# Queries and keys brought to channels by DMA transposes of bfloat16 parts, in a fused mLSTM and feed-forward kernel

## The chip, the cores and the metric

The kernel runs on 1 core of a Trainium2 chip. Its time is the device time of one execution in microseconds (us), given as the median of several runs. A profile of one more execution says what each engine did: PE is the matrix engine (TensorE; PEld its weight loads), DVE the vector engine, ACT the scalar engine, POOL the GpSimd engine, SP the engine that issues nearly all DMAs here (its queue is shown as SPq).

## The reference

An mLSTM layer in its recurrent form (batch 4, 8 heads, 768 tokens, 40 channels a head), then a feed-forward layer without biases on the 3072 tokens of 320 channels (inner width 2048).

```python
for t in range(S):
    m_new = np.maximum(f_gate[:, :, t] + m, i_gate[:, :, t])
    f_stab = np.exp(f_gate[:, :, t] + m - m_new); i_stab = np.exp(i_gate[:, :, t] - m_new); m = m_new
    C = f_stab[..., None, None] * C + i_stab[..., None, None] * np.einsum('bhd,bhe->bhde', vt, kt)
    n = f_stab[..., None] * n + i_stab[..., None] * kt
    h_tilde = np.einsum('bhde,bhe->bhd', C, qt); nq = np.einsum('bhd,bhd->bh', n, qt)[..., None]
    y[:, :, t] = sigmoid(o_gate[:, :, t]) * h_tilde / np.maximum(np.abs(nq), 1.0)
x = y.transpose(0, 2, 1, 3).reshape(B * S, H * D)
h = x @ w_in
out = (np.maximum(h, 0.0) + alpha * np.minimum(h, 0.0)) @ w_out
```

## The kernel before

The recurrence is computed in chunks of 128 tokens: 6 chunks (`NC`) for each of 4 batches, so chunks n = 0 to 23, with c = n % 6 the place in the batch. In a chunk the scores of all 8 heads are a product of keys and queries over the 40 channels (`pS`), weighed by the decays `E`, and multiplied by the values (`pH`). What came before the chunk enters by the state `C_t` (keys by values, 40 x 42 a head: 40 values, and two columns for the denominator), multiplied by the queries (`pI`, none where c is 0); `update` brings the state on (`pu`, none where c is 5). Two chunks make a group g of 256 tokens; the feed-forward of a group runs in 8 steps `fp`: `up` (16 matmuls of 256 columns into `ph`, of an activation and weights that are each split into a high and a low part), ACT and DVE form the activation, ACT and POOL split it (`gh`, `gl`), and two steps later `down` (12 matmuls of 320 columns into `po`).

The Python generators set only the order in which the program is written: `attention` yields pieces, and `side.until` places them between the feed-forward's steps. A scheduler then fixes one order for each engine, and every engine works through its own order strictly in sequence. On SP that goes for DMAs too: a DMA whose wait is not over holds all DMAs behind it.

Queries and keys arrive by token, `qn_t` and `kn_t` of [128 tokens, 8 heads, 64], two buffers each. The matmuls contract over partitions, so both are brought to channels in `stage_a`: four transposes of pairs of heads each (`transposed`, L176: `pq` and `pk` in PSUM), in float32. Up to chunk 6 (`NDIR` is 7) the result is used in float32. From chunk 7 on `stacked` makes of each a stack of 120 partitions: the high part rounded to float32r by ACT (`qh`, `kh`, L184), the rest by DVE or POOL (`kl`, `ql`), and six DMAs of 40 partitions by 512 elements each (L192) lay high, low and high below one another, so that one float32r matmul a head (L369) gives the scores to nearly float32. For the state product the queries are also kept in float32 (`qf`, L221), and `from_state` does two heads at a time in float32 (L302: four matmuls, each seen by the profile as two).

From chunk 8 on (`NBF`) scores and values are split into three bfloat16 parts for `pH` (`score_parts`, `value_parts`, `values_by_parts`). `open_gate` (L119) takes the sigmoid of the output gates of a whole batch; it stands behind the last chunk of the batch before, right after the DMAs that load the gates.

Of the kernel before, what the change touches and what calls it, by code (L numbers as in the profile page):

```python
# [8 lines left out]
F32 = mybir.dt.float32  # L9
# [8 lines left out]
def kernel(ctx: ExitStack, tc: tile.TileContext, q, k, v, i_gate, f_gate, o_gate, w_in, w_out, alpha, out):  # L18
# [59 lines left out]
    wT = const.tile([P, NC, BH], F32, tag="wT", name="wT")  # L78
    ones = const.tile([BH, R], F32, tag="ones", name="ones")
# [9 lines left out]
    def load_qk(n):  # L89
        b, c = divmod(n, NC)  # L90
        t0 = c * P
        nc.sync.dma_start(qn_t[n % NQ][:, :, :D], q[b, :, t0 : t0 + P, :].rearrange("h p d -> p h d"))
        nc.sync.dma_start(kn_t[n % NQ][:, :, :D], k[b, :, t0 : t0 + P, :].rearrange("h p d -> p h d"))

# [33 lines left out]
    def weighed(n):  # L128

        b, c = divmod(n, NC)  # L130
        kd = sb.tile([P, H, D], F32, tag="kd", name=f"kd{n}")
        (nc.gpsimd if n in KDP else nc.vector).tensor_tensor(
            kd, kn_t[n % NQ][:, :, :D], wT[:, c, b * H : (b + 1) * H].unsqueeze(2).broadcast_to([P, H, D]), ALU.mult
        )
        kds[n] = kd
# [6 lines left out]
    def update_steps(n):  # L142
# [9 lines left out]
        for h in range(H):  # L152
            r = slice(64 * (h % 2), 64 * (h % 2) + D)
            nc.tensor.matmul(pu3[r, h], kd[:, h], va[:, h], start=True, stop=True)  # L154
        yield
        old, new = C_t[(n - 1) % 3], C_t[n % 3]
        if c > 0 and n in CP:
# [13 lines left out]
        yield  # L171

    def transposed(ps, src):
        src = src.rearrange("p h e -> p (h e)")
        for p in range(NPR):
            nc.tensor.transpose(ps[:R, p * P : (p + 1) * P], src[:, p * P : p * P + R], ident)  # L176

    def stacked(ps, nm, n, low, copy=None):


        X = sb.tile([3 * D, 2, 512], F32R, tag=f"{nm}S", name=f"{nm}S{n}")
        Xh = sb.tile([P, 512], F32R, tag=f"{nm}h", name=f"{nm}h{n}", bufs=1)
        Xl = sb.tile([P, 512], F32R, tag=f"{nm}l", name=f"{nm}l{n}", bufs=1)
        nc.scalar.copy(Xh[:R], ps[:R])  # L184
        if copy is not None and n in QLP:
            nc.gpsimd.tensor_tensor(Xl[:R], copy[:R], Xh[:R].bitcast(F32), ALU.subtract)
        else:
            nc.vector.tensor_tensor(Xl[:R], ps[:R], Xh[:R].bitcast(F32), ALU.subtract)
        for par in range(2):
            for j in range(3):  # L190
                src = (Xl if j == low else Xh)[64 * par : 64 * par + D]
                nc.sync.dma_start(X[j * D : (j + 1) * D, par].bitcast(F32), src.bitcast(F32))  # L192
        return X

# [18 lines left out]
    def stage_a(n):  # L213

        c = n % NC
        pq = psa(f"pq{n}")
        transposed(pq, qn_t[n % NQ])
        Q = K = qf = None
        if c > 0 or n < NDIR:
            qf = sb.tile([P, 512], F32, tag="qf", name=f"qf{n}")  # L220
            nc.scalar.copy(qf[:R], pq[:R])  # L221
        if n >= NDIR:
            Q = stacked(pq, "q", n, 1, qf)
        yield
        pk = psa(f"pk{n}")
        transposed(pk, kn_t[n % NQ])
        if n >= NDIR:
            K = stacked(pk, "k", n, 2)
        else:
            K = padded(n)  # L230
            padded_copy(K, pk)
        chunk[n] = (pre.pop(n), Q, K, qf)
        yield
        update(n)
        if n >= NBF:
            for _ in value_parts(n):
                pass
        yield

# [54 lines left out]

    def from_state(n, qf):

        b, c = divmod(n, NC)
        pI = psa(f"pI{n}")
        C = C_t[(n - 1) % 3][:R].rearrange("p h e -> p (h e)")
        for p in range(NPR):  # L300
            es = slice(2 * p * VA, 2 * (p + 1) * VA)
            nc.tensor.matmul(pI[:, es], qf[:R, p * P : (p + 1) * P], C[:, es], start=True, stop=True)  # L302
# [37 lines left out]
    def stage_b(n):  # L340

        b, c = divmod(n, NC)
        Lb, Q, K, qf = chunk.pop(n)
        Es = []
        for par in range(2):
# [9 lines left out]
            for p in range(NPR):  # L355
# [7 lines left out]
                compare_op=ALU.is_ge, fill=0.0,  # L363
            )
            pS = psa(f"pS{n}_{par}")
            for p in range(NPR):
                sl = slice(p * P, (p + 1) * P)
                if n >= NDIR:
                    nc.tensor.matmul(pS[:, sl], K[:, par, sl], Q[:, par, sl], start=True, stop=True)  # L369
                else:  # L370
                    nc.tensor.matmul(pS[:, sl], K[:R, par, sl], qf[:R, sl], start=True, stop=True)
# [8 lines left out]
        if c > 0:  # L380
            *_, T = from_state(n, qf)
        hv = values(n, Es) if n < NBF else values_by_parts(n, Es)
# [55 lines left out]
    def attention(n0):  # L438

        late = iter(())  # L440
        for _ in stage_a(n0):
            yield
        for n in range(n0, B * NC):
            loads(n + 2)
            a = stage_a(n + 1) if n + 1 < B * NC else iter(())
            bb = stage_b(n)
            for part in (a, bb, late, a, bb, a, bb):
                next(part, None)
                if part is not late:
                    yield  # L450
            if n % GC == GC - 1:
                late = stage_x(n // GC)
        for _ in late:
            yield
# [11 lines left out]
    XNP = range(2, 8)  # L466
    QLP = range(6, 24)
    KDP = range(1, 24)
# [11 lines left out]
    class FeedForward:  # L480
# [9 lines left out]
        def up(self):  # L490
# [24 lines left out]
            if g == 1:  # L515
                gh, gl = (
                    sb.tile([P, 2, GT], F32R, tag="qk"[fp % 2] + x, name=f"g{x}{g}_{fp}", bufs=1) for x in "hl"
                )
            else:
# [198 lines left out]
    def first_group():  # L718
# [31 lines left out]
        nc.gpsimd.memset(ones, 1.0)  # L750
        for C in C_t:
# [103 lines left out]
        def warm(n=1):  # L855
# [7 lines left out]
        lf = [  # L863
            sb.tile([P, 512], F32, tag="qk"[j] + "h", name=f"g_lf{j}", bufs=1)[:BH, : (GT, S - GT)[j]] for j in range(2)
        ]
# [159 lines left out]
        )  # L1025
        pg = psa("pg")
        nc.tensor.matmul(pg[:R, : BH * NC], ones, gd.rearrange("p a c -> p (a c)"), start=True, stop=True)
        nc.vector.tensor_copy(gamB[:R].rearrange("p a c -> p (a c)"), pg[:R, : BH * NC])
# [90 lines left out]
```

## Time and profile before

| | us |
|---|---|
| three runs | 515.08, 519.91, 520.13; median 519.91 |
| profiled execution | 517.3 |
| its span, first to last instruction | 515.6 |
| PE busy in the span | 497.3 (96%) |
| DVE, ACT, POOL busy | 340.1, 307.2, 243.6 |
| first and last score matmul from stacks (L369) | starts at 144.2 and 443.7 |

Matmuls are pipelined: the duration of one in the profile (0.27 us for a transpose) is longer than the time until the next one starts. What a group of matmuls costs PE is therefore read from start to start.

### The profile page before, as it was taken

Reading aid. Unit: us, or ns where it says so; the run is one execution under the profiler, and the core shown is the slowest. Engines: PE = TensorE matmul, PEld = TensorE weight load, DVE = VectorE, ACT = ScalarE, POOL = GpSimd, SP = SyncE. Lnnn points to the kernel's source line nnn. Section 1 sums busy time; section 2 is a strip of 40 time slices with the busy share of each in tenths; the row PEclk is TensorE's granted clock in tenths of the full one; section 3 lists DMA queues with packets and bytes.
Section 4 is the critical chain, followed back from the end, with each engine's and each line's share of the span. In section 5 each row is a group of like instructions: output and inputs, shape, how many; then the busy total and the mean of one; then the engine's idle time right before and its main releaser. Section 6 shows DMA issues by size and latency. Waiting matters only on the chain.

```text
span 515.6 us, 11550 instructions
## 1 busy us (share of the span) xinstructions
PE 497.3 (96%) x4335; PEld 483.4 (94%) x4335; DVE 340.1 (66%) x667; ACT 307.2 (60%) x638; POOL 243.6 (47%) x286
## 2 busy tenths in 40 slices
PE   8889889999999999999899999999999999999997
PEld 7778879999999999999799999999999999999997
DVE  7879999745544777773586686685786587552321
ACT  3868697545456566574885666566875664433332
POOL 6632362210276366554666647464766645333242
PEclk9989988999999999999899999999999999999999
DMA  9989986070265454367356464356543121000000
GB/s 171 230 179 270 236 207 176 3 144 27 63 168 138 117 147 111 88 161 140 78 160 133 110 146 130 96 132 132 144 129 99 65 77 40 1 27 0 27 1 26
DMA packets 137999, 58.39 MB, mean 113 GB/s; under 512 B 102792, under 2 KB 126360, under 8 KB 137944
## 3 DMA queue, kind: packets, MB, share of 16 engines
q1 hardware_dynamic: 137864, 57.56, 46.4%
q8 instruction: 34, 0.56, 0.5%
q14 instruction: 21, 0.17, 0.1%
q10 hardware_dynamic: 80, 0.11, 0.1%
HBM read 36.90 MB, written 4.03 MB: 79 GB/s over the span
## 4 chain that ended last, share of the span: by engine, by line
PE 76%; DVE 7%; ACT 5%; DMA 4%; issue 3%; SPq 2%; POOL 2%; ACTq 0%; DVEq 0%; POOLq 0%
PE po L530 28%; PE ph L499 4%; PE ph L502 4%; PE ph L503 4%; PE ph L506 4%; PE ph L500 4%; PE ph L505 4%; PE ph L501 4%; PE ph L504 4%; PE pI L302 3%; DMA og<-in_o_gate_dram 3%; PE pH L285 3%; PE pS L369 2%; SPq L115 2%; PE pu L154 2%
## 5 line engine op out<-in xcount | busy, mean ns | idle before, releaser
L522 POOL TENSOR_TENSOR gl<-g,gh 128x512 fp32r<-128x512 f32 x80 | 103.5, 1295 | 76.0 <-ACT gh L521 64.4
L530 PE MATMUL po<-OH,gh 128*128 128x320 f32 x384 | 116.7, 316 | 1.6 <-ACT gh L521 1.6
L530 PE MATMUL po<-OL,gh 128*128 128x320 f32 x384 | 114.4, 310 | 0.0
L512 DVE SCALAR_TENSOR_TENSOR g<-g,oma,ph 128x256 f32<-128x256 f32 x160 | 69.5, 475 | 62.7 <-ACT g L508 62.2
L508 ACT ACTIVATE g<-ph 128x512 f32<-128x512 f32 x96 | 57.5, 599 | 65.7 <-PE ph L506 60.8
L521 ACT CAST gh<-g 128x512 fp32r<-128x512 f32 x80 | 49.6, 620 | 51.8 <-DVE g L512 51.1
L530 PEld LDWEIGHTS po<-OH,gh 128*128 128x128 f32 x384 | 72.4, 189 | 2.4 <-ACT gh L521 2.1
L530 PE MATMUL po<-OH,gl 128*128 128x320 f32 x384 | 73.6, 312 | 0.0
L530 PEld LDWEIGHTS po<-OL,gh 128*128 128x128 f32 x384 | 72.4, 189 | 0.2 <-DVE OL L629 0.2
L530 PEld LDWEIGHTS po<-OH,gl 128*128 128x128 f32 x384 | 60.0, 188 | 0.4 <-POOL gl L522 0.2
L499 PE MATMUL ph<-XH,WH 128*128 128x256 f32 x192 | 59.4, 309 | 0.0
L357 ACT ACTIVATE E<-Lb,bT 128x128 f32<-128x128 f32 x160 | 49.9, 392 | 15.8 <-PE pH L285 13.8
L503 PE MATMUL ph<-X,W 128*128 128x256 f32 x192 | 54.8, 287 | 0.0
L501 PE MATMUL ph<-XH,WL 128*128 128x256 f32 x192 | 54.6, 285 | 0.0
L506 PE MATMUL ph<-X2L,W 128*128 128x256 f32 x192 | 54.5, 285 | 0.0
L500 PE MATMUL ph<-XH,WH 128*128 128x256 f32 x192 | 54.5, 284 | 0.0
L502 PE MATMUL ph<-XH,WL 128*128 128x256 f32 x192 | 54.4, 284 | 0.0
L505 PE MATMUL ph<-XL,WH 128*128 128x256 f32 x192 | 54.3, 283 | 0.0
L504 PE MATMUL ph<-XL,WH 128*128 128x256 f32 x192 | 54.3, 283 | 0.0
L272 ACT CAST E<-pS 128x512 bf16<-128x512 f32 x64 | 37.5, 585 | 19.7 <-DVE pS L270 10.3
L361 POOL TENSOR_SCALAR_AFFINE_SELECT E<-E 128x512 f32<-128x512 f32 x44 | 31.2, 712 | 36.2 <-ACT E L357 35.2
L499 PEld LDWEIGHTS ph<-XH,WH 128*128 128x128 f32 x192 | 36.7, 191 | 0.7
(177 smaller groups left out, 1114.0 us busy)
## 6 DMA issues: line engine op xcount, KB each, us to landing
Lb<-L_d SPq DMA_DIRECT2D x20, 512.0 KB
qS<-qh SPq DMA_DIRECT2D x68, 80.0 KB
kS<-kh SPq DMA_DIRECT2D x68, 80.0 KB
wo<-in_moe_w_out_dram SPq DMA_DIRECT2D x8, 640.0 KB
wi<-in_moe_w_in_dram SPq DMA_DIRECT2D x8, 512.0 KB
qn<-in_q_dram SPq DMA_DIRECT2D x24, 160.0 KB
kn<-in_k_dram SPq DMA_DIRECT2D x24, 160.0 KB
va<-in_v_dram SPq DMA_DIRECT2D x24, 160.0 KB
```

The source lines that it names most:

```text
L499: nc.tensor.matmul(dst, WH[half][:, 0, hs], XH[:, 0], start=True, stop=False)
L500: nc.tensor.matmul(dst, WH[half][:, 1, hs], XH[:, 1], start=False, stop=False)
L501: nc.tensor.matmul(dst, WL[half][:, 0, hs], XH[:, 0], start=False, stop=False)
L502: nc.tensor.matmul(dst, WL[half][:, 1, hs], XH[:, 1], start=False, stop=False)
L503: nc.tensor.matmul(dst, W2[:, fs], X2, start=False, stop=False)
L504: nc.tensor.matmul(dst, WH[half][:, 0, hs], XL[:, 0], start=False, stop=False)
L505: nc.tensor.matmul(dst, WH[half][:, 1, hs], XL[:, 1], start=False, stop=False)
L506: nc.tensor.matmul(dst, W2[:, fs], X2L, start=False, stop=True)
L508: nc.scalar.activation(gt, ph, AF.Relu, scale=-1.0)
L512: nc.vector.scalar_tensor_tensor(out=y[:, e], in0=gt[:, e], scalar=oma[:, f : f + 1], in1=ph[:, e], op0=ALU.mult, op1=ALU.add)
L522: (nc.vector if g < 2 else nc.gpsimd).tensor_tensor(gl, y, gh.bitcast(F32), ALU.subtract)
L530: nc.tensor.matmul(po[j], x[:, e, j * P : (j + 1) * P], W[f // NB][:, f % NB], **ends)
```

## The change

From chunk 7 on TensorE transposes nothing for queries and keys. `stage_s(n + 2)`, two chunks ahead, splits each of them by token into three bfloat16 parts in one tile `Z` of [128 tokens, 2 blocks, 8 heads, 128 places], each block holding 3 x 40 channels and 8 zeros. One DMA transpose on SP's queue turns the 16 blocks of 128 x 128 into a stack `X` of [128 places, 16, 128 tokens] of bfloat16 (512 KB). Block 0 and block 1 hold the parts in two orders, such that two bfloat16 matmuls of 120 partitions a head, block 1 - s of one stack against block s of the other, give six of the nine products of parts.

From batch 1 on the state is kept on 40 partitions (one buffer, `C_t[0]`, updated in place), split into three bfloat16 parts, and laid out as a stack by three plain DMAs (L207 to L209); `from_state` then does two bfloat16 matmuls of 42 columns a head with the query stack. The state of chunk n is split for n = 6 to 22 without c = 5, so 15 times. `qf` is no longer made from chunk 7 on. `open_gate(b)` moves into the first chunk of batch b itself. The feed-forward of group 1 uses the tiles `sp0`, `sp1` that later hold `Z`; `Z` has one buffer for queries and one for keys.

```diff
-    def stacked(ps, nm, n, low, copy=None):
-        X = sb.tile([3 * D, 2, 512], F32R, tag=f"{nm}S", name=f"{nm}S{n}")
...
-                nc.sync.dma_start(X[j * D : (j + 1) * D, par].bitcast(F32), src.bitcast(F32))
+    def token_parts(n, j):
+        src = by_token_of(n, j)
+        Z = sb.tile([P, 2, H, P], BF16, tag=f"sp{j}", name=f"{'qk'[j]}Z{n}", bufs=1)
+        rest = sb.tile([P, H, D], F32, tag="qf", name=f"{'qk'[j]}r{n}")
...
+        nc.gpsimd.memset(Z[:, :, :, 3 * D :], 0.0)
...
+        nc.scalar.copy(both, src.unsqueeze(1).broadcast_to([P, 2, H, D]))
+        (nc.gpsimd, nc.vector)[j].tensor_tensor(rest, src, slot(0, 0), ALU.subtract)
+        yield
+        nc.scalar.copy(slot(1, 1), rest)
+        nc.vector.tensor_tensor(slot(0, 2), rest, slot(1, 1), ALU.subtract)
+        nc.vector.tensor_copy(slot(1 - j, 1 - (1 - j)), slot(0, 0))
+        nc.vector.tensor_copy(slot(j, 1 - j), slot(1, 1))
+        X = sb.tile([P, 2 * H, P], BF16, tag="qk"[j] + "S", name=f"{'qk'[j]}S{n}")
+        nc.sync.dma_start_transpose(X, flat)
...
+    def state(n, pu):
...
+        nc.scalar.copy(X[:D, 0], C)
+        nc.vector.tensor_tensor(rest, C, X[:D, 0], ALU.subtract)
+        nc.scalar.copy(X[:D, 1], rest)
+        nc.gpsimd.tensor_tensor(low, rest, X[:D, 1], ALU.subtract)
+        nc.sync.dma_start(X[D : 2 * D], X[:D])
+        nc.sync.dma_start(X[2 * D : 3 * D, 1], X[:D, 0])
+        nc.sync.dma_start(X[2 * D : 3 * D, 0], low)
...
+            for h in range(H):
+                es = slice(h * VA, (h + 1) * VA)
+                for s in range(2):
+                    nc.tensor.matmul(pI[:, es], Q[: 3 * D, s, h], C[:, 1 - s, es], start=s == 0, stop=s == 1)
...
-                    nc.tensor.matmul(pS[:, sl], K[:, par, sl], Q[:, par, sl], start=True, stop=True)
+                    for s in range(2):
+                        nc.tensor.matmul(
+                            pS[:, sl], K[: 3 * D, 1 - s, h], Q[: 3 * D, s, h], start=s == 0, stop=s == 1
+                        )
...
+            if c == 0 and par == 1:
+                open_gate(b)
...
-            open_gate(b + 1)
...
-            a = stage_a(n + 1) if n + 1 < B * NC else iter(())
+            a = stage_a(n + 1) if n + 1 < NDIR else iter(())
+            far = stage_s(n + 2) if NDIR <= n + 2 < B * NC else iter(())
-            for part in (a, bb, late, a, bb, a, bb):
+            for part in (a, bb, late, far, a, bb, far) + ((a, bb) if n + 1 < NC else (bb, a)):
```

Where the scheduler puts these pieces is seen in the order of each engine. On PE, before, between two steps of group 2's feed-forward (`po2` is the end of one `down`, `ph2_6` the next `up`) stand the query transposes of chunk 9 and half the scores of chunk 8:

```order
L530 MATMUL po2_0_1711<-OH1_873,gl2_3_1927 128x320
L530 MATMUL po2_1_1712<-OH1_873,gl2_3_1927 128x320
L176 MATMUL pq9_2065<-ident_72,qn1_76 104x128 x4
L369 MATMUL pS8_0_2089<-qS8_1792,kS8_1845 128x128 x4
L499 MATMUL ph2_6_2100<-XH2_1683,WH1_553 128x256
```

At the same place now (lines are those of the changed kernel) stand the state update of chunk 8 and twice as many score matmuls, each with a weight load of its own (four of the eight pairs are shown):

```order
L608 MATMUL po2_1_1707<-OH1_871,gl2_3_1927 128x320
L161 MATMUL pu8_2065<-va0_79,kd8_2063 40x42 x8
L443 LDWEIGHTS kS8_1773
L443 MATMUL pS8_0_2103<-qS8_1750,kS8_1773 128x128
L443 LDWEIGHTS kS8_1773
L443 MATMUL pS8_0_2103<-qS8_1750,kS8_1773 128x128
L443 LDWEIGHTS kS8_1773
L443 MATMUL pS8_0_2103<-qS8_1750,kS8_1773 128x128
L443 LDWEIGHTS kS8_1773
L443 MATMUL pS8_0_2103<-qS8_1750,kS8_1773 128x128
```

The transposes are gone there and nothing takes their place; no row of `pq` or `pk` is left from chunk 7 on.

On SP, before, one chunk (17) takes its loads and twelve copies of stack parts:

```order
L99 DMA va0_79<-in_v_dram 128x8x40
L192 DMA qS17_4264<-qh17_4265 40x512 x3
L192 DMA qS17_4264<-ql17_4266 40x512 x2
L192 DMA qS17_4264<-qh17_4265 40x512
L106 DMA Lb19_4577<-L_d_89 128x8x128
L93 DMA kn1_78<-in_k_dram 128x8x40
L99 DMA va0_79<-in_v_dram 128x8x40
L192 DMA kS17_4387<-kh17_4388 40x512 x2
```

Now the same chunk stands there with two transposes, and the three DMAs of the state of chunk 16 behind them:

```order
L244 DMA_TRANSPOSE qS17_4250<-qZ17_4212 128x16x128
L93 DMA kn1_78<-in_k_dram 128x8x40
L244 DMA_TRANSPOSE kS17_4363<-kZ17_4217 128x16x128
L113 DMA Lb19_4727<-L_d_88 128x8x128
L208 DMA C2_87<-C2_87 40x336
L93 DMA qn0_75<-in_q_dram 128x8x40
L207 DMA C2_87<-C2_87 40x672
L106 DMA va0_79<-in_v_dram 128x8x40
L93 DMA kn0_77<-in_k_dram 128x8x40
L209 DMA C2_87<-cw16_4379 40x336
```

The loads of the next chunks (`qn`, `kn`, `Lb`) now stand behind transposes, and each transpose behind the DVE and ACT work on its `Z`.

On ACT, now, the first parts of chunk 10 are written into `Z` between the pieces of group 2's feed-forward step 4:

```order
L427 ACTIVATE E9_1_2449<-Lb9_1799,bT_81 128x128 x4
L235 CAST qZ10_2171<-qn0_75 128x2x8x40
L587 ACTIVATE g2_4_2000<-ph2_4_1983 128x512
L235 CAST kZ10_2176<-kn0_77 128x2x8x40
L599 CAST gh2_4_2004<-g2_4_2000 128x512
L587 ACTIVATE g2_5_2037<-ph2_5_2020 128x512
```

Since `Z` has one buffer, both `L235` rows wait until the transposes of chunk 9 have read it, and `gh2_4` stands behind them.

More of the change, by code (lines that the diff above doesn't have):

```diff
@@ L226, in stage_a, with after @@
         transposed(pk, kn_t[n % NQ])
[L227 to L232, printed above, removed]
+        padded_copy(K, pk)
+        chunk[n] = (None, K, qf)
         yield
+        after(n)
+        yield
+    def after(n):
         update(n)
@@ L237, in stage_a, with stage_s @@
                 pass
+    def stage_s(n):
+        parts = [token_parts(n, j) for j in range(2)]
+        for it in parts:
+            next(it)
+        yield
+        next(parts[0])
+        yield
+        next(parts[1])
+        chunk[n] = (stacks.pop((n, 0)), stacks.pop((n, 1)), None)
         yield
@@ L444, in attention @@
             loads(n + 2)
[L445 removed]
+            a = stage_a(n + 1) if n + 1 < NDIR else iter(())
+            far = stage_s(n + 2) if NDIR <= n + 2 < B * NC else iter(())
             bb = stage_b(n)
[L447 removed]
+            for part in (a, bb, late, far, a, bb, far) + ((a, bb) if n + 1 < NC else (bb, a)):
                 next(part, None)
[L449 removed]
+                if part in (a, bb):
                     yield
+            next(far, None)
+            if NDIR <= n + 1 < B * NC:
+                after(n + 1)
             if n % GC == GC - 1:
@@ L466 @@
     XNP = range(2, 8)
-    QLP = range(6, 24)
     KDP = range(1, 24)
@@ L515, in up @@
             if g == 1:
-                gh, gl = (
-                    sb.tile([P, 2, GT], F32R, tag="qk"[fp % 2] + x, name=f"g{x}{g}_{fp}", bufs=1) for x in "hl"
-                )
+                both = sb.tile([P, 2, 2, GT], F32R, tag=f"sp{fp % 2}", name=f"gg{g}_{fp}", bufs=1)
+                gh, gl = both[:, 0], both[:, 1]
             else:
@@ L863, in first_group @@
         lf = [
-            sb.tile([P, 512], F32, tag="qk"[j] + "h", name=f"g_lf{j}", bufs=1)[:BH, : (GT, S - GT)[j]] for j in range(2)
+            sb.tile([P, 512], F32, tag=f"sp{j}", name=f"g_lf{j}", bufs=1)[:BH, : (GT, S - GT)[j]] for j in range(2)
         ]
```

83 lines of the change are left out of this document (53 added, 30 removed).

## The prediction, written before the changed kernel ran

> **What bounds the kernel now.** I read the busy times first, then the windows (busy us of each engine in a stretch, with the number of instructions), then PE's timeline from start to start.
>
> ```profile
> PE 497.3 (96%) x4335; PEld 483.4 (94%) x4335; DVE 340.1 (66%) x667; ACT 307.2 (60%) x638; POOL 243.6 (47%) x286
> 45.00:110.00 65.00, 60.41 (x494) 57.74 (x493) 57.12 (x108) 48.14 (x107) 22.21 (x27) 0.95 0.70 165
> 145.00:445.00 300.00, 296.96 (x2708) 291.90 (x2707) 207.13 (x400) 190.64 (x406) 171.16 (x193) 0.99 0.46 116
> L369 PE MATMUL pS<-qS,kS 120*128 120x128 f32 x136 | 20.0, 266 | 0.0
> ```
>
> The change touches chunks 7 to 23: 136 score matmuls of 8 a chunk make 17 chunks, and they run from 144 to 444 us. In just this stretch PE is busy 296.96 of 300 us at a granted clock of 0.99, while DVE has 207.13 (69%), ACT 190.64 (64%) and POOL 171.16 (57%). So in the stretch that changes, PE sets the pace; a us of PE work that goes there shortens the run by a us, as long as no other engine steps in. The window 45 to 110 shows what stepping in looks like: DVE at 57.12 of 65 (88%), and PE at 60.41 (93%).
>
> **PE's part of the sum.** These rows are start, duration, line, tile and count; the cost of a group is from its start to that of the next one.
>
> ```profile
> 302.27 0.60 PE L176 MATMUL pq<-ident,qn 128*104 128x128 f32 x4
> 302.71 1.02 PE L302 MATMUL pI<-C,qf 104*128 104x84 f32 x8
> 303.56 0.54 PE L285 MATMUL pH<-vb,E 128*128 128x42 bf16 x10
> 304.15 0.64 PE L285 MATMUL pH<-vb,E 128*128 128x126 bf16 x12
> 304.64 0.36 PE L500 MATMUL ph<-XH,WH 128*128 128x256 f32 x1
> 308.24 0.56 PE L369 MATMUL pS<-qS,kS 120*128 120x128 f32 x4
> 308.63 0.34 PE L499 MATMUL ph<-XH,WH 128*128 128x256 f32 x1
> 43.38 0.38 PE L351 MATMUL pb<-LP,pick 96*128 96x128 bf16 x4
> 43.62 0.38 PE L499 MATMUL ph<-XH,WH 128*128 128x256 f32 x1
> ```
>
> Transposes removed: four take 302.71 - 302.27 = 0.44 us; two such groups in each of 17 chunks: 17 x 0.88 = **-15.0**.
>
> Scores: eight float32r matmuls now, two groups of 308.63 - 308.24 = 0.39, so 0.78 us a chunk. Afterwards 16 bfloat16 matmuls of 128 columns with a weight load each. The nearest row is `pb`, bfloat16 with 96 rows and 128 columns: four in 43.62 - 43.38 = 0.24, 0.06 each, so 0.96. That is 17 x 0.18 = **+3.1**.
>
> State product: 303.56 - 302.71 = 0.85 us now. Afterwards 16 bfloat16 matmuls of 42 columns. The nearest rows are twelve `pH` matmuls of 126, 84 and 42 columns in 304.64 - 304.15 = 0.49: 0.041 each if the weight loads set the pace (16 make 0.65), or 0.49 / 1008 columns x 42 = 0.020 each if columns do (0.33). I take 0.030, 0.48 a chunk, as both kinds stand in that group: 15 chunks have a state product, 15 x 0.37 = **-5.5** (bounds -3.0 and -7.8).
>
> Together -17.4 (-14.9 to -19.7).
>
> **The sigmoid of the gates.** In the trace, ACT waits for a DMA at the second of the three late places:
>
> ```profile
> 243.04 1.28 ACT L119 ACT_TABLE_LOAD   x1 [3.99 <-DMA og<-in_o_gate_dram]
> 246.93 0.57 ACT L415 CAST XH<-p 128x512 fp32r<-128x512 f32 x1
> 248.28 0.67 PE L154 MATMUL pu<-va,kd 128*40 128x42 f32 x16 [2.53 <-DVE XL L418]
> ```
>
> ACT stands 3.99 us for the gates' DMA, its next work (`XH`) is late, DVE's `XL` behind it too, and PE idles 2.53 us. With `open_gate` a chunk later the data lies there: **-2.5**. What is late next at that place is nothing that the trace shows; 0 if some other wait fills the gap.
>
> **The transposes.** No row shows one. They move 512 KB each from SBUF to SBUF. Nearest rows, of SP's queue:
>
> ```profile
> 306.39 2.28 SPq L192 DMA_DIRECT2D qS<-qh  x3
> 311.09 0.43 SPq L106 DMA_DIRECT2D Lb<-L_d  x1
> 305.46 0.84 SPq L99 DMA_DIRECT2D va<-in_v_dram  x1
> qS<-qh SPq DMA_DIRECT2D x68, 80.0 KB
> 258.82 0.87 DVE L563 COPY ob<-po 128x320 f32<-128x320 f32 x2
> 298.07 0.88 DVE L563 COPY ob<-po 128x320 f32<-128x320 f32 x2
> ```
>
> A plain load of as many bytes (`Lb`, 512 KB) holds the queue 0.43 us; the six copies that one transpose replaces (480 KB) hold it 6 x 0.76 = 4.6 us. I take 4.6, the row of the same direction and size, with 0.43 as the lower end and no row for an upper one. A chunk takes 19.6 us (two chunks between the `ob` rows, 39.25). Of it SP needs, at 0.43 to 0.84 an issue, some 2.5 us for loads and stores, 2.3 for the three state DMAs at 0.76, and 9.2 for two transposes: 14.0, not more than the 9.1 + 2.5 of before by much, and it fits. The work they wait for and the work that waits for them (scores) stand some four feed-forward steps apart in PE's order from chunk 8 on, about 14 us. Not so at the start: chunk 7's second half of the scores stands one `up` behind the DVE work that completes `kZ7`. There PE waits for the transpose once: **+4.6** (0.4 to whatever a transpose takes).
>
> [...]
>
> **The other engines.** Rows of the same sizes:
>
> ```profile
> L384 DVE TENSOR_TENSOR T<-T,S 128x336 f32<-128x336 f32 x14 | 11.9, 853 | 0.4
> L384 DVE TENSOR_TENSOR T<-T,pH 128x336 f32<-128x336 f32 x5 | 2.5, 502 | 1.3 <-PE pH L249 1.2
> L924 DVE COPY L_rest<-L 32x256 f32<-32x256 f32 x1 | 0.3, 280 | 0.0
> L563 DVE COPY ob<-po 128x320 f32<-128x320 f32 x22 | 9.9, 479 | 7.6 <-PE po L530 7.6
> L188 DVE TENSOR_TENSOR kl<-pk,kh 104x512 fp32r<-104x512 f32 x17 | 11.6, 684 | 3.6 <-ACT kh L184 3.3
> L625 ACT CAST OH<-t_wo 128x640 fp32r<-128x640 f32 x8 | 5.9, 738 | 2.3 <-DVE t_wo L617 2.0
> L259 ACT CAST vb<-va 128x336 bf16<-128x336 f32 x16 | 7.7, 479 | 0.0
> L184 ACT CAST kh<-pk 104x512 fp32r<-104x512 f32 x17 | 10.1, 592 | 3.4 <-PE pk L176 3.4
> L132 POOL TENSOR_TENSOR kd<-kn,wT 128x320 f32<-128x320 f32 x19 | 14.5, 766 | 45.6 <-DMA kn<-in_k_dram 27.3 <-DVE wT L776 7.9 <-PE pH L285 6.5
> L186 POOL TENSOR_TENSOR ql<-qf,qh 104x512 fp32r<-104x512 f32 x15 | 20.1, 1343 | 31.3 <-ACT qh L184 31.3
> ```
>
> ACT, a chunk: two double casts (0.74 each), two single ones and two of the state (0.48), 3.4, for three of 0.59 that go: 1.6 more, 27 in all, 218 of some 280. POOL: a subtraction of 0.77 and one of the state, two small fills, for `ql` of 1.34: about 0.7 more, 12 in all. Both have room.
>
> DVE does not have much. A chunk gets three subtractions, one of the state (15 of 17 chunks) and four bfloat16 copies of 320 elements, and loses `kl`. A subtraction of two SBUF operands took 0.85 in the late stretch and 0.50 where one operand was in PSUM. A copy is bounded by 0.28 (256 elements, SBUF) and 0.48 (320 from PSUM); I take 0.35. So 3 x 0.85 + 0.75 + 4 x 0.35 - 0.68 = 4.0 us a chunk, 68 in all (39 with 0.50 and 0.28, 77 with 0.85 and 0.48). DVE would have 275 of about 283 us where it had 207 of 300. The order on DVE puts this work between the feed-forward's pairs (`g`, L512), and PE waits for those through `ph` and `gh`. In the window 45 to 110, with DVE at 88%, PE idled 4.6 of 65 us, 7%; at that share the stretch would lose 20 us, but part of those waits came from loads and short chains. I take a loss of 3%, **+8** (0 to 20).
>
> Sum against the profiled execution (517.3, which is 515.6 of span and 1.7 around it, and 2.6 below the median of the runs, 519.91): 517.3 - 17.4 - 2.5 + 4.6 + 8 = 510; with the transposes anywhere below 4.6 a little less. **I forecast 508.**
>
> **Rivals.**
>
> *DVE hides its work after all.* The waits of DVE in the stretch are mostly for PE, and they shrink by themselves when there is more to do. Then the 8 is 0 and the start costs a us or two: 517.3 - 17.4 - 2.5 + 1 = 498.
>
> *DVE becomes the bound.* It decides from 283 - 207 = 76 us of added DVE work in the stretch, 4.5 us a chunk; my upper price is 77. DVE never ran at more than 88% in a long window with this code; 207 + 77 = 284 at 93% is 305 us in place of 300, so 517.3 + 5 - 2.5 = 520: no change, within 512 to 525. Against it: the price at 0.85 already holds the waits for POOL. [...]
>
> *The transposes hold the queue.* Mechanism: SP works in order, and `Z` has one buffer, so ACT's next cast into `Z` waits for the transpose, and `gh` behind it, and PE's `po` behind that. Point: SP is full when two transposes take 18.6 - 4.8 = 13.8 us, 6.9 each. Every us more costs 2 us a chunk, 34 in all: at 8 us 517.3 - 2.5 + 17 x (16.0 + 4.8 - 19.6) = 535, at 10 us 603. For it: no row shows a transpose, and nothing bounds it from above. Against: the same bytes went through the same queue in 9.1 us a chunk. [...]
>
> That the change does not do what it says can be left out: no row of `pq` or `pk` is left in PE's order.
>
> **How the numbers follow.** My forecast (500 to 513) gets 0.46, DVE hidden (about 498) 0.10, DVE bound 0.19, transposes in the way 0.25. A measurement of this kernel can tell about 1% from no change, 5 us: faster means below 514.7. The first two are faster, the third the same, the last slower: 0.56, 0.19, 0.25. The range leaves out the best end of the second and transposes of over 8 us: 496 to 540.
>
> **What would show it.** PE's rows L176 gone from chunk 7 on, score groups of about 0.24 per four matmuls, state products of 0.3 to 0.65. DVE's share in the stretch of the scores: under 92% with PE at 97% or more for the forecast; over 95% with PE waiting for `gh` or `ph` for the second rival. On SP's queue the time of L244: under 5 us each for the forecast; over 7, with ACT's waits L235 behind the transposes, for the third. I am wrong in the sum if the new small matmuls take over 0.1 us each, and in the reasons if PE is full and the time the same.

## The result, and the profile after

The changed kernel takes 545.29 us (four runs, 543.58 to 546.0) against 518.12 for the one before on the same chip: a ratio of 1.0525, with an interval of 1.0456 to 1.0593. It is slower by 5%, where faster by 2% was forecast. The profiled execution took 543.6, its span 541.9.

The changed kernel's page, busy times (with share of the span) and the chain that ended last:

```profile
PE 496.4 (92%) x4455; PEld 473.2 (87%) x4455; DVE 403.2 (74%) x782; ACT 326.7 (60%) x687; POOL 265.8 (49%) x336
...
PE 23%; DVE 20%; DMA 10%; ACT 7%; issue 3%; POOL 2%; ACTq 0%; POOLq 0%; SPq 0%; DVEq 0%
```

Windows of it, two in the stretch with the scores and a short one ahead of it (us of the window, then busy us of PE, PEld, DVE, ACT and POOL, the granted clock, the DMA share, GB/s):

```profile
145.00:445.00 300.00, 271.70 (x2616) 258.73 (x2615) 248.51 (x469) 196.15 (x428) 180.40 (x226) 0.96 0.63 122
400.00:445.00 45.00, 39.84 (x366) 38.06 (x365) 36.56 (x67) 28.97 (x65) 25.48 (x32) 0.89 0.36 71
126.00:129.00 3.00, 3.00 (x17) 2.91 (x17) 0.69 (x1) 0.61 (x2) 0.00 (x0) 0.50 0.66 129
```

In the same 300 us PE had 296.96 us of work before and has 271.70 now. No other engine is full either: DVE has 248.51 (83%). So nothing became the bound; the engines wait for each other, and DMAs now stand in the chain with 10% (4% before).

The granted clock is lower as well: 0.96 in these 300 us, 0.89 in the last 45, against 0.99 before. It is not lower throughout. The trace has it at 0.50 for some 3 us at a time, as in the window from 126 us, which stands behind an idle time of PE of 4.49 us. In that window the matmuls of `ph` start 0.21 us apart (126.17, 126.39, 126.60); at 190.58 and 190.69 it is 0.11. Of PE's eleven idle times of over 1.5 us between 100 and 450 us, seven stand beside such a piece and four do not, and from 300 to 350 us, with PE busy 44.58 of 50, the clock was 1.00. So an idle time alone does not tell when it comes. By the mean clock of the two profiled executions (0.986 in 515.6 us, 0.962 in 541.9) PE lacked some 7 us of full speed before and some 21 now. The difference, 13 us, is an estimate of the most that this took of the 26 us between the two spans. No experiment separates it from the idle time that it goes with.

PE's own work shrank as planned. Start, duration, line, count in the changed kernel:

```profile
155.41 0.57 PE L372 MATMUL pI<-C,qS 120*128 120x42 bf16 x16
155.83 1.96 PE L312 MATMUL pH<-va,E 128*128 128x42 f32 x16
...
165.53 0.62 PE L443 MATMUL pS<-qS,kS 120*128 120x128 bf16 x8
165.96 0.36 PE L578 MATMUL ph<-XH,WH 128*128 128x256 f32 x1
```

Half the scores of a chunk cost 165.96 - 165.53 = 0.43 us (0.39 before), a state product 0.42 (0.85 before). With the 0.88 of the transposes that is 17 x (0.88 - 0.08) + 15 x 0.43 = 20 us less for PE. They are more than lost in two kinds of gaps.

**The landing of the transposes.** The longest waits (in total, times, longest, us) that end with a transpose's landing, and one that hangs on them:

```profile
ACT kZ L235 <- DMA kS<-kZ: 17.4, 11, 3.0
POOL qZ L231 <- DMA qS<-qZ: 15.7, 8, 6.7
...
DVE kZ L241 <- ACT kZ L235: 15.3, 10, 2.9
POOL kZ L231 <- DMA kS<-kZ: 14.5, 6, 5.0
...
ACT qZ L235 <- DMA qS<-qZ: 8.0, 8, 1.9
```

One of these places in the timeline, engine by engine (SP's queue, ACT, POOL, DVE, PE; in brackets the idle time ahead and what ended it):

```profile
217.47 2.07 SPq L244 DMA_TRANSPOSE kS<-kZ  x1
219.64 3.37 SPq L244 DMA_TRANSPOSE qS<-qZ  x1
...
223.27 0.72 ACT L235 CAST kZ<-kn 128x640 bf16<-128x640 f32 x1 [2.86 <-DMA kS<-kZ]
...
223.30 0.20 POOL L231 MEMSET kZ<- 128x128 bf16 x1 [5.03 <-DMA kS<-kZ]
223.74 1.26 POOL L600 TENSOR_TENSOR gl<-g,gh 128x512 fp32r<-128x512 f32 x1 [0.23 <-POOL kZ L231]
...
224.03 1.08 DVE L241 COPY kZ<-kZ 128x320 bf16<-128x320 bf16 x1 [2.39 <-ACT kZ L235]
...
222.76 0.30 PE L608 MATMUL po<-OL,gh 128*128 128x320 f32 x1
225.06 0.90 PE L608 MATMUL po<-OH,gl 128*128 128x320 f32 x2 [1.99 <-POOL gl L600]
```

`kZ` has one buffer. The transpose that reads it is issued at 217.47, holds SP's queue for 2.07 us, and has landed at about 223.2, where the waits for it end. Until then POOL stands for 5.03 us before a fill of 0.20 us, with `gl` behind it; ACT for 2.86 before its cast; DVE for 2.39 before a copy that needs the cast; and PE for `gl`. From a transpose's issue to ACT's next cast into the same tile it is 4.3 us at the least, and in the median 4.9 (queries) and 5.8 us (keys). In the 35 waits of ACT and POOL that a landing ended, it came 4.3 to 6.8 us after the issue: the casts stand right at the landing.

**DVE held by POOL.** The other kind, at 190 us, in the same view (POOL, DVE, PE):

```profile
189.75 1.08 POOL L206 TENSOR_TENSOR cw<-cw,C 40x336 bf16<-40x336 f32 x1
190.79 0.72 POOL L401 TENSOR_TENSOR og<-og,r 128x320 f32<-128x320 f32 x1
191.47 0.77 POOL L326 TENSOR_TENSOR vb<-vr,vb 128x336 bf16<-128x336 f32 x1
192.21 1.28 POOL L600 TENSOR_TENSOR gl<-g,gh 128x512 fp32r<-128x512 f32 x1
...
190.52 3.31 DVE L239 TENSOR_TENSOR qZ<-qr,qZ 128x320 bf16<-128x320 f32 x1
193.76 0.23 DVE L242 COPY qZ<-qZ 128x320 bf16<-128x320 bf16 x1
193.91 0.68 DVE L333 TENSOR_TENSOR pS<-pS,E 128x512 f32<-128x512 f32 x1
194.51 0.85 DVE L591 SCALAR_TENSOR_TENSOR g<-g,oma,ph 128x256 f32<-128x256 f32 x2
...
195.42 0.38 PE L578 MATMUL ph<-XH,WH 128*128 128x256 f32 x1 [2.08 <-DVE g L591]
```

One subtraction of 320 elements takes 3.31 us: it ends only after POOL's row of four instructions, which follow one another without a pause. The shortest of its kind took 0.48, in the view of lines (ns, shortest, median, longest; then the first and the last start):

```profile
L239 DVE TENSOR_TENSOR qZ<-qr,qZ x17: 476/969/3950, 117.6 to 435.6; 128x320 bf16<-128x320 f32 x17
```

Of the 134 instructions that the change gives DVE for the parts of queries, keys and state, the 50 with no POOL instruction beside them take at most 1.06 of the shortest of their kind; the 84 with one take 2.1 of it in the median and up to 8.3. Together they took 91 us, 44 more than if each had taken the shortest. Behind the held one stand `g`, and PE's next `ph`.

### The profile page after: what moved, and what is told of

The parts are those of the page before. It is cut to its first block, busy times and chain, and to the rows that moved or that the text cites. A ratio compares the mean times of both kernels' runs of the same rounds, so it can differ in the third digit from the quotient of the medians.

```text
span 541.9 us, 11795 instructions
## 1 busy us (share of the span) xinstructions
PE 496.4 (92%) x4455; PEld 473.2 (87%) x4455; DVE 403.2 (74%) x782; ACT 326.7 (60%) x687; POOL 265.8 (49%) x336
## 4 chain that ended last, share of the span: by engine, by line
PE 23%; DVE 20%; DMA 10%; ACT 7%; issue 3%; POOL 2%; ACTq 0%; POOLq 0%; SPq 0%; DVEq 0%
PE po L608 11%; DMA kS<-kZ 6%; DMA qS<-qZ 3%; DVE qZ L239 3%; DVE g L591 3%; DVE pS L333 2%; PE ph L578 1%; PE ph L580 1%; ACT E L427 1%; PE ph L581 1%; PE ph L584 1%; PE ph L582 1%; PE ph L583 1%; PE ph L585 1%; PE ph L579 1%
## 5 line engine op out<-in xcount | busy, mean ns | idle before, releaser
L600 POOL TENSOR_TENSOR gl<-g,gh 128x512 fp32r<-128x512 f32 x80 | 106.0, 1327 | 88.8 <-ACT gh L599 72.6
L608 PE MATMUL po<-OH,gh 128*128 128x320 f32 x352 | 109.5, 323 | 5.1 <-ACT gh L599 5.1
L608 PE MATMUL po<-OL,gh 128*128 128x320 f32 x352 | 106.8, 315 | 0.3 <-DVE OL L707 0.3
L591 DVE SCALAR_TENSOR_TENSOR g<-g,oma,ph 128x256 f32<-128x256 f32 x160 | 69.3, 472 | 44.1 <-ACT g L587 43.7
L608 PEld LDWEIGHTS po<-OH,gh 128*128 128x128 f32 x352 | 67.8, 193 | 5.9 <-ACT gh L599 5.7
L608 PE MATMUL po<-OH,gl 128*128 128x320 f32 x352 | 70.9, 323 | 2.2 <-POOL gl L600 2.2
L608 PEld LDWEIGHTS po<-OL,gh 128*128 128x128 f32 x352 | 67.7, 193 | 0.5 <-DVE OL L707 0.5
L608 PEld LDWEIGHTS po<-OH,gl 128*128 128x128 f32 x352 | 56.5, 194 | 2.6 <-POOL gl L600 2.5
L431 POOL TENSOR_SCALAR_AFFINE_SELECT E<-E 128x512 f32<-128x512 f32 x44 | 32.4, 738 | 53.5 <-ACT E L427 51.0
L581 PE MATMUL ph<-XH,WL 128*128 128x256 f32 x192 | 55.7, 290 | 0.0
L584 PE MATMUL ph<-XL,WH 128*128 128x256 f32 x192 | 55.6, 290 | 0.0
L583 PE MATMUL ph<-XL,WH 128*128 128x256 f32 x192 | 55.4, 289 | 0.0
L580 PE MATMUL ph<-XH,WL 128*128 128x256 f32 x192 | 55.4, 289 | 0.0
```

The lines of the kernel that those rows point to most:

```text
L580: nc.tensor.matmul(dst, WL[half][:, 0, hs], XH[:, 0], start=False, stop=False)
L581: nc.tensor.matmul(dst, WL[half][:, 1, hs], XH[:, 1], start=False, stop=False)
L583: nc.tensor.matmul(dst, WH[half][:, 0, hs], XL[:, 0], start=False, stop=False)
L584: nc.tensor.matmul(dst, WH[half][:, 1, hs], XL[:, 1], start=False, stop=False)
L591: nc.vector.scalar_tensor_tensor(out=y[:, e], in0=gt[:, e], scalar=oma[:, f : f + 1], in1=ph[:, e], op0=ALU.mult, op1=ALU.add)
L600: (nc.vector if g < 2 else nc.gpsimd).tensor_tensor(gl, y, gh.bitcast(F32), ALU.subtract)
```

## The experiments

Ratios are to the kernel before, run on the same chip. The changed kernel stands at 1.0525. Each edit lets the scheduler order all engines anew. One small edit near the end of this section made the kernel 9 us slower, and why is not known. So a single difference of that size proves little; several of 20 us that point the same way prove more.

**Taking one or the other away.**

The first edit leaves out the transposes (`NDIR + 2` is 9) and uses old stacks again, the second leaves out DVE's low part and copies (`NKEEP` is 9). Parts of the edits are left out here.

```diff
+        if n < NDIR + 2:
...
+            nc.sync.dma_start_transpose(X, flat)
...
+        if n <= NKEEP:
+            nc.vector.tensor_tensor(slot(0, 2), rest, slot(1, 1), ALU.subtract)
+            nc.vector.tensor_copy(slot(1 - j, 1 - (1 - j)), slot(0, 0))
+            nc.vector.tensor_copy(slot(j, 1 - j), slot(1, 1))
```

> Leaves out the DMA transposes from chunk 9 on (the stacks of chunks 7 and 8 are used again); everything that fills Z stays. Two theories. LANDING: Z has one buffer, so ACT's cast, POOL's fill and what is queued behind them on both engines wait for the last transpose to land (ACT's casts into Z waited 25.4 us, POOL's fills 30.2 us in the changed kernel). It expects most of the 27 us back: 520 to 525 us against 545. HOLD: DVE's new instructions with two SBUF operands, and its bfloat16 copies, wait while POOL has an instruction running (one subtraction of 0.48 us took 3.95 us), and g and the scores wait behind them in DVE's order. It expects little: 538 to 543 us, DVE's subtraction for qZ still at a mean near 1.4 us, PE still with gaps of over 2 us that end with g.

> Leaves out DVE's low part and two copies for each of qZ and kZ from chunk 10 on (Z keeps old values there); casts, fills, the remainders and the transposes stay. HOLD: DVE loses some 46 us of the 54 that these instructions take, and the gaps behind them: 520 to 525 us. LANDING: ACT's and POOL's waits for the landing stay, and with less to do DVE waits more: 538 to 543 us.

> Leaves out both: no transposes from chunk 9 on, no DVE low parts and copies for Z from chunk 10 on. Both theories expect what the matmul side of the prediction gave, 517 less 17 plus a few us for the casts, the remainders and the state's parts that are left: 502 to 510 us. If it stays above 515, something else in the change (the state's parts, the clock of TensorE, the place of the sigmoid) costs as much, and neither theory is the whole.

Measured: without transposes 525.67 us, 1.0173 (1.0092 to 1.0253); without DVE's parts 526.76, 1.0168 (1.0084 to 1.0251); without both 512.03, 0.9912 (0.9874 to 0.9949). Neither theory is the whole. Each cure gives back some 18 us, both 32; 512.03 is a little over what the third expectation allowed for (510).

**The work moved**, the low parts to POOL and the copies to ACT:

```diff
-        nc.vector.tensor_tensor(slot(0, 2), rest, slot(1, 1), ALU.subtract)
+        nc.gpsimd.tensor_tensor(slot(0, 2), rest, slot(1, 1), ALU.subtract)
...
-        nc.vector.tensor_copy(slot(1 - j, 1 - (1 - j)), slot(0, 0))
-        nc.vector.tensor_copy(slot(j, 1 - j), slot(1, 1))
...
+        nc.scalar.copy(slot(1 - j, 1 - (1 - j)), slot(0, 0))
+        nc.scalar.copy(slot(j, 1 - j), slot(1, 1))
```

> Computes all that the changed kernel computes, but the low parts of qZ and kZ on POOL and the two copies of each on ACT. HOLD: DVE is rid of 54 us, POOL gets two subtractions of 0.8 us a chunk (27 us, to some 290), ACT four copies of 0.46 (31 us, to some 358): 522 to 530 us. LANDING: Z is filled no earlier and lands no earlier, and ACT and POOL, which do the waiting, have more to do: 545 to 555 us.

Measured: 520.79 us, 1.0083 (1.0042 to 1.0123). That is what the theory of the hold expected (522 to 530) and a little better, though POOL still waits 28.8 us for landings there and ACT 16.1 (30.2 and 25.4 in the changed kernel).

**Held, or too much?** The same number of DVE instructions for each `Z`, with one operand in PSUM. `plus(to, x)` adds on DVE a zero that lies in 160 columns of `po`'s bank, which DVE clears once a group (ten instructions more in all):

```diff
+            plus(slot(0, 2), slot(1, 1))
+            plus(slot(1 - j, 1 - (1 - j)), slot(0, 0))
+            plus(slot(j, 1 - j), slot(1, 1))
```

> The changed kernel, but from chunk 11 on the low part and the two copies of each Z are additions of a zero that lies in PSUM, on DVE as before (the low part so becomes the middle part again, no matter here). DVE's instructions and elements are as many; with one operand in PSUM they should take about 0.5 us each whatever POOL does, so 6 of them some 3.0 us a chunk, against 3.6 in the changed kernel. Two readings of HOLD are told apart. If it is the coupling to POOL that costs (one instruction standing for up to 4 us ahead of g), 528 to 534 us. If it is the amount of DVE's work, little changes: 539 to 545 us.

Measured: 527.05 us, 1.0118 (1.005 to 1.0186). All 78 of them, in that kernel (shortest, median, longest ns), and its window of the stretch:

```profile
L247 DVE TENSOR_TENSOR qZ<-qZ,po x39: 470/477/482, 203.8 to 427.4; 128x320 bf16<-128x320 bf16 x39
L247 DVE TENSOR_TENSOR kZ<-kZ,po x39: 426/478/489, 209.4 to 432.1; 128x320 bf16<-128x320 bf16 x39
...
145.00:445.00 300.00, 283.12 (x2785) 270.66 (x2784) 250.09 (x507) 209.37 (x453) 187.20 (x239) 0.99 0.62 125
```

None takes over 0.49 us, with POOL busy 187.20 of the 300 us. DVE is as busy in the 300 us as without this edit (250.09 us against 248.51), and the waits for landings are still there (POOL 25.8 us, ACT 21.9), yet 4 points of the 5.25% go. So it is the coupling to POOL that costs, not the amount. The trace of the changed kernel agrees. Of the 160 `g` (L591, with `ph` in PSUM), 68 begin while POOL has an instruction running and take 419 to 482 ns; the other 92 take 459 to 482. Of the 17 subtractions for `qZ` (L239, both operands in SBUF), the ten that begin so take 928 to 3950 ns, the other seven 476 to 493. What couples the two engines is not shown.

**Out of the landing's way.** First by writing the three pieces of `stage_s` one place later, in the changed kernel and in the one with the work moved, and there also without the fills:

```diff
-            for part in (a, bb, late, far, a, bb, far) + ((a, bb) if n + 1 < NC else (bb, a)):
+            for part in (a, bb, late, a, bb, far) + ((a, bb, far) if n + 1 < NC else (bb, far, a)):
```

> The changed kernel with the three pieces of work on chunk n+2 each one place later: the casts into Z and the fills stand two feed-forward steps further behind the last transposes (some 13 us instead of 6.5). LANDING: the waits of ACT and POOL for the landing vanish as they did without transposes, and the run gives back about what that gave (20 us): 524 to 532 us. HOLD alone: the same instructions stand beside the same POOL work: 540 to 546 us.

> Both cures in a kernel that computes all: low parts of Z on POOL, its copies on ACT, and the three pieces one place later. If HOLD and LANDING are two separate losses, the second cure still gives part of its 20 us here (the waits for the landing left in the version with the first cure alone are 50 us on POOL and ACT together): 508 to 514 us against 521. If what is left there is the load of ACT and POOL, nothing changes: 519 to 523 us.

> As the one before, and Z is kept from chunk 9 on, so POOL fills its unused columns no more (two instructions a chunk, 0.2 us each, and their place in POOL's order ahead of gl). With the pieces later there is no landing to wait for: it expects 0 to 3 us less, 507 to 513 us. If POOL's fills still wait for transposes, 5 us or more.

Measured: 544.33 us, 1.052 (1.045 to 1.0589); 527.06, 1.02 (1.0149 to 1.0252); 523.98, 1.014 (1.0097 to 1.0182). This told nothing of the landing, since the edit did not move what it was to move: the scheduler put the casts back. With the shift alone it is still 4.9 and 5.6 us in the median from a transpose to the next cast, and on ACT 16 (queries) and 11 (keys) instructions from the last cast of one chunk to the first of the next, as in the changed kernel. 544.33 lies where the hold alone was expected, but for this reason; the other two lie above all their ranges. Why the shift made the version with the work moved slower (1.02 against 1.0083) is not known.

Then with the first piece of `stage_s` (fills, casts, remainders) bound in the order in which it is written. `queue` ties these instructions, on each engine, behind the last one written ahead of them there; that fixes an order and adds no wait:

```diff
+        start = len(nc.cur_bb.bb.instructions)
+        last = {}
+        for i in nc.cur_bb.bb.instructions[:start]:
+            last[i.engine] = i
         for it in parts:
             next(it)
+        queue(start, len(nc.cur_bb.bb.instructions), last)
```

> The changed kernel with the three pieces one place later as before, and this time ACT's casts into Z and POOL's fills are bound behind the instruction that was written ahead of them on their engine (the plain shift left the casts of a chunk one to eight instructions behind the last ones of the chunk before on ACT; now it is some fifteen). LANDING: by the time of a cast the last transpose has landed, the 25 us of ACT's and 30 us of POOL's waits for it go below 10 each, and the run comes near the one without transposes: 525 to 532 us. If the transposes cost through their traffic or through SP's queue, or only HOLD counts, it stays at 538 to 546 us.

> The changed kernel with ACT's casts into Z and POOL's fills bound behind what was written ahead of them on their engine, and the three pieces at their old place. If the binding does it, casts come 8 us or more after the transposes before and the run takes 515 to 522 us, as with the shift. If the shift is needed, the casts still stand at the landing: 530 to 545 us.

> The binding of the run before in the version with Z's low parts on POOL and its copies on ACT. If HOLD and LANDING are separate losses, this brings both cures together: 508 to 515 us, against 521 for the first cure alone. If ACT and POOL are now so full that what is gained on landing is lost there, 518 to 524 us.

> As the one before, with the remainder of kZ on POOL too. DVE loses 16 subtractions with a mean of 0.98 us there (held up to 2.7), POOL gets 16 of 0.8: HOLD expects 2 to 5 us less than the one before. If POOL is full enough that gl comes later, 0 to 4 us more.

Measured: bound and a place later 516.7 us, 0.9959 (0.9922 to 0.9995); bound alone 517.32, 1.0029 (0.999 to 1.0068). The binding by itself gives back 5 of the 5.25%, 26 us, and no instruction is left out or changed. In it a cast comes 11.0 and 10.6 us after the transpose in the median (21 instructions on ACT). What is left of the waits for a landing at `Z`, above 2 us in total, with the binding alone:

```profile
POOL qZ L231 <- DMA qS<-qZ: 7.6, 4, 2.5
...
POOL kZ L231 <- DMA kS<-kZ: 2.1, 2, 1.4
```

And its window of the stretch:

```profile
145.00:445.00 300.00, 290.18 (x2871) 278.43 (x2870) 252.89 (x511) 211.12 (x459) 191.47 (x244) 0.99 0.64 125
```

PE has 290.18 of 300 us again, DVE even a little more than in the changed kernel (252.89 against 248.51), and the clock is back at 0.99. The binding does not change the casts alone, since the scheduler orders the rest around them: the instructions that the change gives DVE stand only 26 us above their shortest there, against 44.

With the work moved as well it was 519.42, 1.0037 (0.9998 to 1.0076), and with the remainder of the keys on POOL too 517.93, 1.0017 (0.9978 to 1.0055). So the two cures do not add, and the expectation of 508 to 515 was wrong. Its other half, 518 to 524, held. Either moving DVE's work gains nothing once little waits for a landing, or what it gains is lost again to the load of ACT and POOL (in the 300 us ACT has 234.49 us there and POOL 215.93, against 214.01 and 193.26 in the bound order without it). The runs do not tell these apart.

**The transposes' traffic**, in the bound order a place later:

> The bound order without the transposes from chunk 9 on (old stacks are used again). In the order of the changed kernel that gave 20 us. If all of it was the wait for the landing: 514 to 518 us, no less than the bound version with its transposes. If traffic or SP's queue counts: 505 to 511 us.

Measured: 515.52 us, 0.9977 (0.9936 to 1.0018), the same as with them (0.9959) to within some 3 us, by the intervals. So in this order the transposes cost nothing that shows. The 18 us that they cost in the changed kernel were hardly their traffic or their time on SP's queue; the wait for their landing is what is left.

A second buffer for `Z`, which would take that wait away without any binding, was not tried.

**The start.** In the changed kernel PE stands still at chunk 7:

```profile
119.42 2.65 SPq L244 DMA_TRANSPOSE qS<-qZ  x1
...
124.11 0.59 ACT L599 CAST gg<-ph 128x512 fp32r<-128x512 f32 x1 [2.39 <-DMA qS<-qZ]
...
125.47 0.39 PE L578 MATMUL ph<-XH,WH 128*128 128x256 f32 x1 [4.49 <-DVE gg L600]
```

The feed-forward of group 1 writes `gg` into the tile that the transpose of `qZ` still reads. A tile of its own for pairs 5 to 7:

```diff
-            if g == 1:
+            if g == 1 and fp < 5:
```

> The bound order, and gh and gl of group 1 leave Z's tiles from pair 5 on (the three buffers of the other groups serve them). In the bound version TensorE stood 6.75 us at 129 us, and gh waited there for the landing of chunk 7's transposes. If that is the cause, the gap goes to 1 to 2 us and the run to 510 to 513 us against 517. If chunk 7 itself is late there (its scores behind its transposes), the gap only moves: 515 to 518 us.

> The changed kernel, and only gh and gl of group 1 leave Z's tiles from pair 5 on. It takes away at most the gap of 4.7 us at 121 us, if that is among the pairs from 5 on: 539 to 543 us. If the loss were mainly the shared tile, 525 us or less.

Measured: in the bound order a place later 508.84 us, 0.9854 (0.9797 to 0.9912), and the gap is gone in which PE stood 6.55 us for `gg` in that order; the 1% from 0.9959 is some 5 us. In the order of the changed kernel alone 544.08, 1.0547 (1.0491 to 1.0603), nothing: the gap stays (`PE ph <- DVE gg` 4.5 us), so the pairs that wait there are earlier ones. That run does not tell what the tile costs in that order.

**More off DVE, in the best order.**

> The run before with the low part of qZ on POOL instead of DVE (DVE less 11 us, POOL 14 more). If held DVE instructions still cost: 2 to 4 us less than the run before. If they don't once nothing waits for a landing: within 2 us of it, or some us more because gl comes later on POOL.

> The run with the bound order and the tile of its own, and the remainder of the state on POOL (DVE less 10 us, POOL 12 more). The state's chain (cast, remainder, cast, low part, three DMAs) then changes engine less often. Held DVE work still costing: 1 to 3 us less. Otherwise within 2 us.

Measured: the state's remainder on POOL 507.37 us, 0.9822 (0.9761 to 0.9883), not to be told from 508.84; the low part of `qZ` on POOL 519.55, 1.0022 (0.9982 to 1.0061), some 9 us worse. The expectation allowed some us, for a later `gl` on POOL; why that one edit costs as much as 9 stays open.

**The sigmoid alone**, in the kernel before:

```diff
+            if c == 0 and par == 1:
+                open_gate(b)
...
             load_gate(b + 1, nc.sync)
-            open_gate(b + 1)
```

> The kernel before with the sigmoid of the gates a place later, as the change has it, and nothing else of it. The prediction put 2.5 us on this step. In the changed kernel PE still idles 2.3 to 2.8 us beside the table load and the sigmoid (3.1 us of ACT), so the second theory is that the place makes no difference: 0. It expects 516 us, the same as before; the first 513.5.

Measured: 515.37 us, 0.9983 (0.995 to 1.0016): between 2.6 us less and 0.8 more, by the interval. Neither expectation is excluded. The changed kernel shows what is late there next:

```profile
255.07 1.28 ACT L126 ACT_TABLE_LOAD   x1
256.37 1.80 ACT L126 ACTIVATE og<-og 128x1920 f32<-128x1920 f32 x1
258.07 0.57 ACT L335 CAST E<-pS 128x512 bf16<-128x512 f32 x1
...
258.70 0.23 PE L348 MATMUL pH<-vb,E 128*128 128x126 bf16 x1 [2.56 <-ACT E L335]
```

## Why the prediction was wrong, step by step

*PE's part, -17.4:* right; 20 us by the rows. The new score matmuls take 0.054 us each (0.06 was taken), those of the state 0.026 (0.030).

*The sigmoid, -2.5:* not shown; alone it measured 0.9 us less, and 2.5 is the far end of the interval. The DMA's wait is gone, but ACT itself is held there for 3.1 us by the table load and the sigmoid, and PE idles 2.56. "Nothing that the trace shows" was late next, the prediction said; the duration of the sigmoid and its table load were in that trace.

*The transposes, 4.6 each on SP's queue:* **the step that failed.** The prediction put the wait of `Z`'s next writers at nothing as long as SP's queue is not full. In the changed kernel ACT waited 25.4 us and POOL 30.2 us for landings, and an order that keeps these writers away from the landing gave back 26 us with every instruction left in. The price on the queue was even too high: 2.6 and 2.0 us in the median.

```profile
L244 SPq DMA_TRANSPOSE qS<-qZ x17: 1624/2632/3684, 119.4 to 441.1; - x17
L244 SPq DMA_TRANSPOSE kS<-kZ x17: 1799/2022/3243, 123.2 to 439.2; - x17
```

The landing came later than that, 4.3 us after the issue at the earliest. But the time on the queue is not what anyone waits for. The prediction looked at the readers of the result (the scores, some 14 us away) and not at the next writers of the source: `Z` has one buffer, and its next fill and cast wait until the transpose has landed. It named this chain in its third rival (ACT's next cast into `Z`, `gh` behind it, `po` behind that), but let it begin only when SP's queue is full, at 6.9 us a transpose. It began where the order put the cast nearer to the transpose than its landing, 4.3 to 6.8 us behind the issue, and that order was there to be read, as ACT's row of instructions. The result lies between the two prices of that rival, 535 and 603, by luck: they stand for transposes of 8 and 10 us on the queue, and none took over 3.7.

*The start, +4.6:* the size came out by luck. It was taken as a time on the queue, which is 2.65 us there; 4.7 us is the time from the transpose's start to that of the cast that waits for its landing. The place was wrong: not the scores wait for the transpose but the feed-forward, for the shared tile.

*DVE, +8 (0 to 20):* the amount was right, 63 us more (403.2 - 340.1) where 68 was said. (The lower price of 39 does not come out of its rows, which give some 45; nothing hangs on it.) The waits for POOL, which the prediction saw in the price of 0.85, are in the trace of the kernel before: of the fourteen additions of two SBUF operands (L384), the ten that begin while POOL has an instruction running take 678 to 1575 ns, the other four 504 to 508. The theory of DVE's cost, by its share of the stretch, was not right. At 83% DVE was below the 92% of the forecast, and lost more. The run with an operand in PSUM shows that the coupling to POOL cost, with the amount unchanged. That the loss is by single instructions that stand for 1.5 to 4 us ahead of `g`, and only if there is no slack, is argued: in the bound order with its own tile these instructions still take 31 us above their shortest, against 44, and the kernel reaches 508.84.

*The clock:* the sum had no term for it. At most 13 us, by the estimate above.

*The sum.* It gave 510 with all terms, against 517.3, a ratio of 0.986. The changed kernel with nothing but the binding measured 1.0029, and 0.9959 a place later: 9 and 5 us above the sum. 0.9854 was measured only with the tile of its own as well, which takes away the start's +4.6 that the sum contains. So it is partly luck that this version's 508.84 stands at the forecast of 508; without the +4.6 the sum is 505.4. What the last us are is not shown. POOL and ACT still wait 14.7 us for landings in that version.

*The signs that were to tell.* They crossed: L244 under 5 us on SP, for the forecast; ACT's waits at L235 behind the transposes, for the third rival; DVE under 92%, but PE at 91% in place of 97%.

How the 27 us divide between landing and hold can't be given as a sum. One cure alone gives 18 to 26 us, both together 25 (moved and bound) to 32 (left out): a hold costs PE little while ACT and POOL are early, and the waits for the landing are what makes them late. That they meet in this way is argued from these ratios; the single runs show only that each cure removes most. The share of the clock is not separated either.

## What to carry to other kernels

For an asynchronous copy or transpose, look at both ends: who reads the result, and who next writes the source. With one buffer the source is taken until the landing, which here came 4.3 to 6.8 us after the issue while the queue was held for 1.6 to 3.7, and an in-order engine that meets that wait passes it on to all that is queued behind it: POOL stood for 5.03 us before a fill of 0.20, with `gl` behind it. Check in each engine's order how far the next writer stands from the transfer; if it is too near, bind it later before taking anything out. Price DVE instructions like these (subtractions of two SBUF operands, bfloat16 copies within SBUF) by what POOL does beside them: the 84 with a POOL instruction beside them took 2.1 of the shortest of their kind in the median, and one stood for a whole row of four POOL instructions, 3.31 us. Where PE begins to idle, read the granted clock in short windows too (here 0.50 for some 3 us at a time): the idle time may not be all that is lost.

## What was not expected of the hardware

Two held DVE subtractions did not get in between POOL instructions that followed one another without a pause: one took 3.31 us over four of them, another 3.95, also over four. It is not always so: the one of 1.25 us at 247.70 us ended while the second of two such POOL instructions still ran. The 34 DMA transposes of 512 KB between SBUF tiles held SP's queue for 1.6 to 3.7 us each, and ACT's next cast into the source came 4.3 us after the issue at the earliest. In the bound order their traffic cost nothing measurable: 0.9959 with and 0.9977 without the transposes. Seven of PE's eleven longer idle times stood beside a piece of some 3 us (once 7) at a granted clock of 0.50.
